# Three pairs of row buffers, a longer lag and a new order in a fused attention and expert kernel

## The chip, the cores and the metric

The kernel runs on one core of one Trainium2 chip. The metric is the device time of one execution in microseconds (us), as the median of the runs shown. The profile is of one further execution; its own time stands beside its span below.

## The reference

Sliding-window attention with a distance bias, then a layer of eight experts whose weights come from eight rounds of row and column balancing. Every token goes through every expert.

```python
q, k, v: (8, 8, 576, 64) float32          # batch, heads, positions, head size
scores = q @ k.T / 8 - slope[head] * |distance|, where 0 <= distance < 128, else -1e9
x = softmax(scores) @ v                    # laid out as (4608, 512)

logits = x @ w_gate                        # (4608, 8)
P = np.exp(logits - logits.max())
for _ in range(8):
    P /= P.sum(1, keepdims=True) + 1e-09
    P /= P.sum(0, keepdims=True) + 1e-09
    P *= N / E
out = 0
for e in range(8):
    h = np.maximum(x @ w1[e], 0.0)         # w1[e]: (512, 1024)
    out += P[:, e:e + 1] * (h @ w2[e])     # w2[e]: (1024, 512)
```

## The kernel before, in words

The kernel schedules itself by hand: the instructions of an engine run in the order in which the program issues them, and an engine that waits holds up what is queued behind it. Semaphores are set from the regions of buffers that are read and written.

The first stage (to about 300 us) is the attention, with the experts 0 and 1 woven in as plain matmuls. Their results go unweighted to a scratch tensor `ysp` in HBM, and the rows of x to another, `xd`. The second stage is the balancing of P. Neither is touched by the change, but for the place of two constants.

The third stage does the experts 2 to 7. Its unit is one group of 256 tokens (two blocks of 128) and one expert: 18 groups of six experts, N = 108 units. `units[n]` gives the group and the expert; the unit's place in its group is n % 6 (NE = 6), place 0 for expert 2 up to place 5 for expert 7. In the first group, experts 6 and 7 (units 4 and 5) run layer 1 plainly. In all others both layers are done by Winograd's form of Strassen's 2x2 product, with seven products in place of eight:

- **Layer 1** (`part`, L983). The x operand of a group is in `xset` (four transposed quarters and four sums of them, made by `sums_x`). The seven products a11, s1, s2, a12, s3, s4, a22 accumulate in three PSUM banks A, B and C, with three copies on ScalarE that carry a partial result on (A to B after a11, C to the SBUF buffer `s5` after s1, B to C after s2). A result is one of four quarters ("slots" 0 to 3) of h. Slot 0 is read from bank A after a12, slot 3 is bank B plus s5 (token `p+`, VectorE, L1027, `add_h`), slot 1 is bank C plus s5 (`c+`), slot 2 is bank B after a22. ScalarE applies the relu with the token's weight P as scale (`relu`, L1013) and leaves 128 x 512 fp16 rows in `hr`.
- **The transposes** (`turn_h`, L1019, issued on SP). `hr` holds four quarters, two pairs: slots 0 and 3, slots 1 and 2. When a pair is complete, one DMA transposes it into `hs[n % 2]`. The same four quarters are written again in the next unit.
- **Layer 2** (`product`, L1071). Five sums of the transposed quarters are made on VectorE (`sum_h`, L1043, tokens t5, t6, t1, t4, t7). The seven products of a unit run in the order 3, 4, 2, 6, 1, 5, 7. Product 3 and product 4 read quarters of the first pair; products 2, 6, 1, 5, 7 read t5, t6, t1, t4, t7. They accumulate over the six experts of a group in PSUM (`sum_of`), in four of five banks that rotate from group to group. Token `X` in a plan is the next product of a single long stream, so the number of X in each plan sets how far layer 2 lags behind layer 1.
- **Gathering** (`gather`, tokens g1 to g7, L1113). When a group's products are complete they are added into `acc`, which `begin` (tokens B0, B1, L1087 and L1091) has started with the weighted results of experts 0 and 1; these come from `ysp` through a buffer y (tokens Y0, Y1, `load_y`, L1081, issued on POOL). `finish` (token FIN) sends acc to the output.
- **The next x** comes by `XL0`, `XL1` (loads from xd on POOL) and `XT0`, `XT1` (transposes on SP), then `SX` (`sums_x`).
- **Weight sums** for the experts (`todo`) are done on VectorE, by tokens W in the first units (`sums_at` says how many at the start of a unit).

A plan is a string of such tokens for one place of a group, written out by hand; `step` carries it out in order:

```python
plans = (
    "a11 X s1 X s2 a12 X s3 p+ s4 c+ t5 X t6 t7 X X t4 a22 X t1",
    ...
```

Token `F` in units 0 and 1 is a piece of the second stage's leftover work. The very last unit has no successor: its layer 2 is done plainly (`plain`, L1133), against rows of expert 7's w2 that are loaded again, because the Strassen sums had replaced a part of them (`load_w2`, eight pieces on POOL).

Of the kernel before, what the change touches and what calls it, by code (L numbers as in the profile page):

```python
# [9 lines left out]
FP16 = mybir.dt.float16  # L10
FP32 = mybir.dt.float32
# [3 lines left out]
def kernel(  # L15
# [10 lines left out]
    nc = tc.nc  # L26
    AF = mybir.ActivationFunctionType
    ALU = mybir.AluOpType
# [52 lines left out]
    ident32 = per.tile([P, P], FP32, name="ident32")  # L81
    ones32 = per.tile([P, P], FP32, name="ones32")
# [169 lines left out]
    if True:  # L252
# [752 lines left out]
        hr = per.tile([P, 4, HF], FP16, name="hr", tag="xT", bufs=4)  # L1005
        hs: dict = {}
        AT = {0: 0, 3: 1, 1: 2, 2: 3}

        def relu(n, slot, src):

            g, e = units[n]
            blk = 2 * g + slot % 2
            nc.scalar.activation(out=hr[:, AT[slot]], in_=src, func=AF.Relu, scale=P_sb[:, blk, e : e + 1])  # L1013

        def turn_h(n, i):

            if n % 2 not in hs:
                hs[n % 2] = per.tile([P, 8, NF2, P], FP16, name=f"hs_{n % 2}", tag="hT", bufs=2)
            nc.sync.dma_start(  # L1019
                out=hs[n % 2][:, 2 * i : 2 * i + 2].rearrange("p s f k -> p (s f) k"),  # L1020
                in_=hr[:, 2 * i : 2 * i + 2].rearrange("p s f -> p (s f)"),
                transpose=True,
            )

        def add_h(n, slot, name):
            to = hr[:, AT[slot]]
            nc.vector.tensor_tensor(out=to, in0=psum(name), in1=s5, op=ALU.add)  # L1027
            relu(n, slot, to)
            if slot == 3:
                turn_h(n, 0)  # L1030
# [52 lines left out]
        def begin(g, e):  # L1083
            for m in range(2):
                blk = 2 * g + m
                if e == 0:
                    nc.vector.tensor_scalar(  # L1087
                        out=acc[:, m, :], in0=y[:, m, :], scalar1=P_sb[:, blk, 0:1], scalar2=None, op0=ALU.mult
                    )
                else:  # L1090
                    nc.vector.scalar_tensor_tensor(  # L1091
                        out=acc[:, m, :], in0=y[:, m, :], scalar=P_sb[:, blk, 1:2], in1=acc[:, m, :],
                        op0=ALU.mult, op1=ALU.add,
                    )
# [32 lines left out]
        def plain(m, name, lo, hi):  # L1127
# [3 lines left out]
            fts = [(f + NF2 * m) % NFT for f in range(NFT)]  # L1131
            for ft in fts:
                nc.tensor.matmul(  # L1133
                    out=ps,
                    lhsT=hs[(N - 1) % 2][:, AT[2 * (ft // NF2) + m], ft % NF2, :],
                    rhs=W2L[e]["all"][:, ft, lo:hi],
                    start=(ft == fts[0]),
                    stop=(ft == fts[-1]),
                )
            a = acc[:, m, lo:hi]  # L1140
# [3 lines left out]
            nc.sync.dma_start(out=out[t0 : t0 + P, lo:hi], in_=a)  # L1144

# [20 lines left out]
        y = s5y[:, 1].bitcast(FP16).rearrange("p (m d) -> p m d", m=2)  # L1166
# [24 lines left out]
        def step(n, plan):  # L1191
            gi = n // NE
            for tok in plan.split():
# [16 lines left out]
                elif tok in ("B0", "B1"):  # L1210
                    begin(groups[gi], int(tok[1]))
# [12 lines left out]
                elif tok in ("Y0", "Y1"):  # L1224
                    load_y(groups[gi], int(tok[1]))
# [15 lines left out]
        )  # L1241
        first = {
# [4 lines left out]
            N - 1: "a11 s1 X B1 s2 X a12 X s3 p+ s4 X c+ t5 X t6 X a22 X t1 t4 g3 X t7 X g4 X g2 X g6 g1 g5 g7",  # L1247
        }
        sums_at = {1: 3, 2: 3, 3: 2, 4: 4, 5: 3, 6: 3, 9: 4, 10: 3}
        for n in range(N):  # L1250
# [3 lines left out]
            if n == 1:  # L1254
# [43 lines left out]
```

## Time and profile before

| | |
|---|---|
| median of 3 runs | 1015.14 us (1015.04 to 1016.08) |
| the profiled execution | 1014.62 us, its span 1012.8 us |
| PE (TensorE matmul) busy | 985.9 us, 97% |
| DVE (VectorE) busy | 685.7 us, 68% |
| ACT (ScalarE) busy | 626.4 us, 62% |
| POOL (GpSimd) busy | 181.0 us, 18% |
| transposes hs<-hr on SP | 216, median 3.2 us from issue to landing |
| loads of y on POOL | 36 of 256 KB, median 3.3 us to landing |
| loads of x rows on POOL | 34 of 128 KB, median 2.7 us to landing |

PEld is the load of TensorE's stationary operand, which runs beside the matmuls. A group line has the line of the kernel, engine, operation and buffers (written<-read), the count, the busy time and the mean of one in ns; a wait line has who waited for whom, us in total, times and the longest. In a timeline line the first two numbers are the start from the span's start and the duration in us, and a square bracket holds the idle time of the engine just before and what ended it. Consecutive instructions of an engine overlap at their ends in this record, so the distance of two starts is what one costs.

### The profile page before, as it was taken

Reading aid. Unit: us, or ns where it says so; the run is one execution under the profiler, and the core shown is the slowest. Engines: PE = TensorE matmul, PEld = TensorE weight load, DVE = VectorE, ACT = ScalarE, POOL = GpSimd, SP = SyncE. Lnnn points to the kernel's source line nnn. Section 1 sums busy time; section 2 is a strip of 40 time slices with the busy share of each in tenths; the row PEclk is TensorE's granted clock in tenths of the full one; section 3 lists DMA queues with packets and bytes.
Section 4 is the critical chain, followed back from the end, with each engine's and each line's share of the span. In section 5 each row is a group of like instructions: output and inputs, shape, how many; then the busy total and the mean of one; then the engine's idle time right before and its main releaser. Section 6 shows DMA issues by size and latency. Waiting matters only on the chain.

```text
span 1012.8 us, 19357 instructions
## 1 busy us (share of the span) xinstructions
PE 985.9 (97%) x7247; PEld 624.6 (62%) x7247; DVE 685.7 (68%) x1546; ACT 626.4 (62%) x1000; POOL 181.0 (18%) x317
## 2 busy tenths in 40 slices
PE   8999999999999999999999999999999999999997
PEld 5645665556544666666666666666666666666655
DVE  5737667665698778676676666666666666677665
ACT  7655645454424656767766666666766666677663
POOL 3324544445100000001000000011100000000011
PEclk9999999999999999999999999999999999999999
DMA  9998899989995656676666655655656656655676
GB/s 244 214 272 219 181 242 222 234 169 183 210 214 130 133 105 131 133 121 125 135 121 125 132 121 120 133 122 120 139 122 124 137 122 130 130 126 120 139 128 115
DMA packets 382877, 155.54 MB, mean 154 GB/s; under 512 B 334720, under 2 KB 372352, under 8 KB 382784
## 3 DMA queue, kind: packets, MB, share of 16 engines
q1 hardware_dynamic: 359680, 110.87, 54.4%
q0 software_dynamic: 22672, 43.27, 19.1%
q8 instruction: 57, 0.93, 0.4%
q14 instruction: 36, 0.29, 0.1%
q10 hardware_dynamic: 432, 0.16, 0.1%
HBM read 78.30 MB, written 23.59 MB: 101 GB/s over the span
## 4 chain that ended last, share of the span: by engine, by line
PE 81%; DMA 11%; DVE 5%; ACT 1%; issue 1%; DVEq 0%; ACTq 0%
PE psM L1071 27%; PE psy L159 12%; PE psB L983 11%; DMA hs<-hr 10%; PE psh L137 9%; PE psA L983 8%; PE psC L983 7%; PE psh L118 3%; DVE hr L1027 2%; PE psS L457 1%; PE psN L491 1%; DMA k<-in_k_dram 1%; DVE hs L1043 1%; DVE pt L468 1%; ACT pt L463 1%
## 5 line engine op out<-in xcount | busy, mean ns | idle before, releaser
L1071 PEld LDWEIGHTS <-hs 128*128 128x128 f16 x2996 | 291.2, 98 | 160.9 <-DVE hs L1043 20.6
L1071 PE MATMUL psM<-w2l,hs 128*128 128x256 f16 x1440 | 216.7, 274 | 12.6 <-DVE hs L1043 11.3
L1013 ACT ACTIVATE hr<-hr,L_sb 128x512 f16<-128x512 f16 x212 | 144.2, 716 | 92.7 <-DVE hr L1027 90.7
L1027 DVE TENSOR_TENSOR hr<-psB,s5y 128x512 f16<-128x512 f32 x106 | 73.3, 692 | 184.2 <-PE psB L983 141.2
L1043 DVE TENSOR_TENSOR hs<-hs 128x512 f16<-128x512 f16 x535 | 192.7, 418 | 1.1 <-DMA hs<-hr 0.4
L983 PEld LDWEIGHTS <-xset 128*128 128x128 f16 x1484 | 144.5, 97 | 76.2 <-issue 4.0
L159 PE MATMUL psy<-w2t,hT 128*128 128x512 f16 x576 | 135.7, 379 | 0.0
L1071 PE MATMUL psM<-more,hs 128*128 128x256 f16 x864 | 126.5, 273 | 0.5 <-DMA hs<-hr 0.5
L983 PE MATMUL psA<-w1l,xset 128*128 128x512 f16 x356 | 105.9, 379 | 0.4 <-ACT hr L1013 0.4
L983 PE MATMUL psB<-s,xset 128*128 128x512 f16 x356 | 105.6, 378 | 0.0
L149 ACT ACTIVATE hT<-psh 128x512 f16<-128x512 f32 (+1 forms) x104 | 60.4, 581 | 70.1 <-PE psh L137 70.0
L137 PE MATMUL psh<-xT,w1t 128*128 128x512 f16 (+1 forms) x448 | 99.0, 364 | 0.0
L463 ACT ACTIVATE pt<-psS 128x1024 f16<-128x1024 f32 x64 | 64.6, 1022 | 50.6 <-PE psS L457 50.1
L1013 ACT ACTIVATE hr<-psA,L_sb 128x512 f16<-128x512 f32 x110 | 76.0, 691 | 26.3 <-DMA hs<-hr 18.3
L159 PEld LDWEIGHTS <-hT 128*128 128x128 f16 x576 | 54.1, 98 | 58.9 <-issue 1.3
L1184 ACT COPY psC<-psB 128x512 f32<-128x512 f32 x106 | 60.4, 570 | 47.3 <-PE psB L983 47.3
L1113 DVE TENSOR_TENSOR acc<-acc,psM 128x256 f32<-128x256 f32 (+1 forms) x162 | 77.4, 506 | 10.5 <-PE psM L1071 7.8
L1027 DVE TENSOR_TENSOR hr<-psC,s5y 128x512 f16<-128x512 f32 x106 | 72.5, 683 | 16.4 <-DMA hs<-hr 12.3
L1180 ACT COPY psB<-psA 128x512 f32<-128x512 f32 x106 | 60.4, 570 | 33.5 <-PE psA L983 33.5
L582 DVE CAST yo<-psy 128x512 f16<-128x512 f32 x65 | 44.6, 689 | 51.2 <-PE psy L159 47.1
L1081 POOL DMA_DIRECT2D s5y<-ysp x36 | 25.9, 720 | 280.7 <-DVE acc L1091 213.5
L1013 ACT ACTIVATE hr<-psB,L_sb 128x512 f16<-128x512 f32 x108 | 72.7, 673 | 2.9 <-PE psB L996 1.1
(133 smaller groups left out, 1167.2 us busy)
## 6 DMA issues: line engine op xcount, KB each, us to landing
s5y<-ysp POOLq DMA_DIRECT2D x36, 256.0 KB, 3.3
ysp<-yo SPq DMA_DIRECT2D x65, 128.0 KB, 4.2
v<-in_v_dram SPq DMA_DIRECT2D x32, 256.0 KB, 4.8
out_dram<-acc POOLq DMA_DIRECT2D x30, 256.0 KB, 3.1
q<-in_q_dram SPq DMA_DIRECT2D x5, 1024.0 KB, 6.6
k<-in_k_dram SPq DMA_DIRECT2D x5, 1024.0 KB, 9.3
xst<-xd POOLq DMA_DIRECT2D x34, 128.0 KB, 2.7
hs<-hr SPq DMA_TRANSPOSE x216, 3.2
```

The costliest lines, as they stand in the source:

```text
L137: nc.tensor.matmul(out=ps[:, 0:nt], lhsT=w1ts[e][:, dt, P * ft : P * ft + P], rhs=xT[:, at : at + nb, dt, :], start=(dt == 0), stop=(dt == ...
L149: nc.scalar.activation(out=st["hT"][:, ft, 0:nt], in_=ps[:, 0:nt], func=AF.Relu)
L159: nc.tensor.matmul(out=ps, lhsT=st["hT"][:, ft, P * ms : P * ms + P], rhs=w2ts[e][:, ft, :], start=(ft == 0), stop=(ft == NFT - 1),)
L463: nc.scalar.activation(out=pt, in_=ps.rearrange("p a y n -> p (a y) n"), func=AF.Exp, scale=scale)
L983: nc.tensor.matmul(out=psum(name), lhsT=xset[n // NE % 2][:, x, P * k : P * k + P], rhs=q[k], start=(start and k == 0), stop=(k == 1), ski ...
L1013: nc.scalar.activation(out=hr[:, AT[slot]], in_=src, func=AF.Relu, scale=P_sb[:, blk, e : e + 1])
L1027: nc.vector.tensor_tensor(out=to, in0=psum(name), in1=s5, op=ALU.add)
L1043: nc.vector.tensor_tensor(out=t[:, AT.get(to, to)], in0=t[:, AT[x]], in1=t[:, AT[y]], op=op)
L1071: nc.tensor.matmul(out=ps, lhsT=hs[n % 2][:, LEFT[m], f, :], rhs=W2L[e][RIGHT[m]][:, f, :], start=(e == 2 and f == 0 and half == 0), stop= ...
L1113: nc.vector.tensor_tensor(out=a, in0=a, in1=p2, op=op)
L1180: nc.scalar.copy(out=psum("B"), in_=psum("A"))
L1184: nc.scalar.copy(out=psum("C"), in_=psum("B"))
```

## The change

- The rows of h: the four quarters of `hr` are cut into two pairs and a third pair is put beside `s5` in the tile `s5y`, where y was. The pair i of unit n is number (2n + i) % 3.
- The lag: unit 1 has two X in place of three. From then on a unit runs five products of the unit before the last and two of the last one. The last unit has twelve.
- y: loaded and used by blocks of 128 tokens (tokens Y00, Y01, Y10, Y11 and B00, B01, B10, B11, expert and block), 72 loads of 128 KB. Three blocks of a group use one buffer `y_e` in turn, in the place that the buffer for x rows had. The x rows' buffer is now the tile of the two constants (identity and ones, no longer needed by then), and the fourth block of y uses it too.
- All plans are written anew: p+ and c+ follow s3 and s4 more closely, the sums t come in another order, the weight sums of unit 0 stand behind its a22, the gathers are drawn from places 1 and 2 mostly into place 1, XL1 follows XT0 at once.
- The plain units 4 and 5 use bank B for slot 2 (before: A).
- The last unit: the plain layer 2 runs in halves, first all that reads the first pair of rows, then all that reads the second; the eight pieces of w2 are loaded in three units (3, 3, 2), not four.

```diff
-    ident32 = per.tile([P, P], FP32, name="ident32")
-    ones32 = per.tile([P, P], FP32, name="ones32")
+    consts = per.tile([P, 2, P], FP32, name="consts")
+    ident32, ones32 = consts[:, 0], consts[:, 1]
...
-        hr = per.tile([P, 4, HF], FP16, name="hr", tag="xT", bufs=4)
+        hr4 = per.tile([P, 4, HF], FP16, name="hr", tag="xT", bufs=4)
+        hr = [hr4[:, 0:2], hr4[:, 2:4]]
...
+        def rows(n, i):
+            return hr[(2 * n + i) % 3]
+        def quarter(n, slot):
+            return rows(n, AT[slot] // 2)[:, AT[slot] % 2]
...
-            nc.scalar.activation(out=hr[:, AT[slot]], in_=src, func=AF.Relu, scale=P_sb[:, blk, e : e + 1])
+            nc.scalar.activation(out=quarter(n, slot), in_=src, func=AF.Relu, scale=P_sb[:, blk, e : e + 1])
...
-                in_=hr[:, 2 * i : 2 * i + 2].rearrange("p s f -> p (s f)"),
+                in_=rows(n, i).rearrange("p s f -> p (s f)"),
...
-            to = hr[:, AT[slot]]
+            to = quarter(n, slot)
...
-        def load_y(g, e):
-            nc.gpsimd.dma_start(out=y, in_=ysp[e, 2 * g : 2 * g + 2].rearrange("m p d -> p m d"))
+        def y_at(e, m):
+            return xst[0] if e == m == 1 else y[0]
+        def load_y(g, e, m):
+            nc.gpsimd.dma_start(out=y_at(e, m), in_=ysp[e, 2 * g + m])
...
-        def plain(m, name, lo, hi):
+        def plain(m, name, fh, lo, hi):
...
-            fts = [(f + NF2 * m) % NFT for f in range(NFT)]
-            for ft in fts:
+            done = name in begun
+            begun.append(name)
+            for f in range(NF2):
...
-        y = s5y[:, 1].bitcast(FP16).rearrange("p (m d) -> p m d", m=2)
+        hr.append(s5y[:, 1].bitcast(FP16).rearrange("p (s f) -> p s f", s=2))
+        y: list = []
...
-                    plain_l1(n, slot, {0: "A", 3: "B", 1: "C", 2: "A"}[slot])
+                    plain_l1(n, slot, {0: "A", 3: "B", 1: "C", 2: "B"}[slot])
...
         plans = (
-            "a11 X s1 X s2 a12 X s3 p+ s4 c+ t5 X t6 t7 X X t4 a22 X t1",
-            "a11 g4 X s1 X g3 s2 g6 X g5 a12 s3 p+ s4 X c+ X X a22 t5 g7 t6 X t4 t1 t7 Y0 XL0",
-            "a11 g2 s1 X g1 FIN X s2 a12 X s3 p+ s4 X c+ X t5 t4 a22 XT0 t6 X X t7 t1 XL1",
-            "a11 X s1 X s2 a12 X s3 p+ s4 c+ X X t5 t6 a22 X XT1 t4 t1 t7 X B0 Y1",
-            "a11 X s1 X s2 a12 X s3 s4 p+ X c+ t5 X a22 X t4 t6 t1 X SX t7",
-            "a11 s1 X X s2 a12 X s3 s4 p+ X c+ X t5 t4 t6 a22 t7 t1 X X B1",
+            "a11 s1 X X s2 X a12 s3 s4 p+ X c+ t5 t6 X a22 X t1 t4 X t7",
+            "a11 s1 X g4 X s2 g3 X a12 g6 s3 X s4 p+ X X c+ a22 g5 X t5 t7 g7 t6 t1 t4 g2 Y00 XL0",
+            "a11 s1 X s2 g1 FIN X X a12 s3 p+ s4 X c+ t5 X a22 XT0 XL1 t6 t1 X X t7 t4",
+            "a11 s1 X X s2 B00 Y01 X a12 s3 s4 p+ c+ t5 X t6 X t4 a22 X t1 X XT1 t7 B01",
+            "a11 Y10 Y11 s1 X X s2 X X a12 s3 p+ s4 c+ X t5 t6 t7 X t4 X a22 t1 SX B10",
+            "a11 X X s1 s2 a12 X X s3 B11 s4 p+ c+ X X X t5 t6 t4 t7 a22 t1",
         )
         first = {
-            0: "a11 s1 W W F s2 a12 F W W s3 p+ s4 c+ F W W a22 F",
-            1: "a11 s1 F s2 a12 F s3 p+ s4 c+ t5 t6 X t1 X t4 a22 X t7 Y0",
-            4: "L0 X X L3 X X L1 t5 X t6 t4 X L2 X SX t7 t1",
-            5: "L0 X X L3 X X L1 t5 X t6 t4 X L2 X B1 t7 t1",
-            N - 1: "a11 s1 X B1 s2 X a12 X s3 p+ s4 X c+ t5 X t6 X a22 X t1 t4 g3 X t7 X g4 X g2 X g6 g1 g5 g7",
+            0: "a11 s1 W W F s2 a12 F s3 s4 p+ c+ F a22 W W F",
+            1: "a11 s1 F s2 a12 F s3 s4 p+ c+ X t5 t6 t1 t4 t7 a22 X",
+            4: "L0 Y10 Y11 X X L3 X X L1 X t5 X t6 t4 L2 t7 t1 X SX B10",
+            5: "L0 X X L3 B11 X X L1 X t5 X t6 t4 L2 t7 t1 X",
+            N - 1: "a11 X s1 s2 a12 B11 X s3 s4 p+ c+ X X a22 X t5 X X t6 t1 t4 g3 X t7 X g4 X g2 X g6 X g1 g5 g7",
         }
-        sums_at = {1: 3, 2: 3, 3: 2, 4: 4, 5: 3, 6: 3, 9: 4, 10: 3}
+        sums_at = {1: 3, 2: 3, 3: 3, 4: 4, 5: 4, 6: 3, 9: 4, 10: 3}
...
-                xst[:] = [per.tile([P, HD], FP16, name="xst", tag="yo", bufs=YO)] * 2
-                step(n, "XL0")
-            if N - NE + 1 <= n < N - 1:
-                for i in range(2):
-                    load_w2(E - 1, 2 * (n - N + NE - 1) + i, 8)
-        plain(1, "A", 0, HD)
-        plain(0, "C", 0, HB)
-        plain(0, "B", HB, HD)
+                y.append(per.tile([P, HD], FP16, name="y_e", tag="yo", bufs=YO))
+                xst[:] = [consts.rearrange("p a n -> p (a n)").bitcast(FP16)] * 2
+                step(n, "Y00 XL0")
+            if N - NE + 1 <= n < N - 2:
+                for i in range(3 * (n - N + NE - 1), min(8, 3 * (n - N + NE))):
+                    load_w2(E - 1, i, 8)
+        plain(1, "A", 1, 0, HD)
+        plain(0, "C", 0, 0, HB)
+        plain(0, "B", 0, HB, HD)
+        plain(1, "A", 0, 0, HD)
+        plain(0, "C", 1, 0, HB)
+        plain(0, "B", 1, HB, HD)
```

More of the change, by code (lines that the diff above doesn't have):

```diff
@@ L1078, in product, with begin @@
                 )
-        def load_y(g, e):
-            nc.gpsimd.dma_start(out=y, in_=ysp[e, 2 * g : 2 * g + 2].rearrange("m p d -> p m d"))
[L1083 to L1094, printed above, removed]
+        def y_at(e, m):
+            return xst[0] if e == m == 1 else y[0]
+        def load_y(g, e, m):
+            nc.gpsimd.dma_start(out=y_at(e, m), in_=ysp[e, 2 * g + m])
+        def begin(g, e, m):
+            blk = 2 * g + m
+            if e == 0:
+                nc.vector.tensor_scalar(
+                    out=acc[:, m, :], in0=y_at(e, m), scalar1=P_sb[:, blk, 0:1], scalar2=None, op0=ALU.mult
+                )
+            else:
+                nc.vector.scalar_tensor_tensor(
+                    out=acc[:, m, :], in0=y_at(e, m), scalar=P_sb[:, blk, 1:2], in1=acc[:, m, :],
+                    op0=ALU.mult, op1=ALU.add,
+                )
         def gather(g, m):
@@ L1125, in finish @@
                         nc.gpsimd.dma_start(out=out[t0 : t0 + TL, :], in_=a[TL * half : TL * half + TL])
-        def plain(m, name, lo, hi):
+        def plain(m, name, fh, lo, hi):
             g, e = units[N - 1]
             ps = psum(name)[:, 0 : hi - lo]
-            fts = [(f + NF2 * m) % NFT for f in range(NFT)]
-            for ft in fts:
+            done = name in begun
+            begun.append(name)
+            for f in range(NF2):
                 nc.tensor.matmul(
                     out=ps,
[L1135 to L1138, printed above, removed]
-                )
+                    lhsT=hs[(N - 1) % 2][:, AT[2 * fh + m], f, :],
+                    rhs=W2L[e]["all"][:, NF2 * fh + f, lo:hi],
+                    start=(not done and f == 0),
+                    stop=(done and f == NF2 - 1),
+                )
+            if not done:
+                return
             a = acc[:, m, lo:hi]
@@ L1209, in step @@
                         gather(groups[last], int(tok[1]))
-                elif tok in ("B0", "B1"):
-                    begin(groups[gi], int(tok[1]))
+                elif tok[0] == "B":
+                    begin(groups[gi], int(tok[1]), int(tok[2]))
                 elif tok == "FIN":
```

5 lines of the change are left out of this document (3 added, 2 removed).

## The prediction

> **What bounds the kernel now.** First the page's busy times and its row of granted clocks, then the waits, then the order of time in one unit that loses time, then the last unit.
>
> ```profile
> PE 985.9 (97%) x7247; PEld 624.6 (62%) x7247; DVE 685.7 (68%) x1546; ACT 626.4 (62%) x1000; POOL 181.0 (18%) x317
> ...
> PEclk9999999999999999999999999999999999999999
> ```
>
> PE is the bound and the others have a third of their time free. So only PE's own pauses can be won. Up to 321 us nothing is changed; all that follows is on the 108 units of the routed stage.
>
> Working of a unit: 7 layer-1 products of 0.43 us (two 512-wide matmuls, the distance of consecutive ones in the timeline) and 7 layer-2 products of 0.437 us (8 matmuls take 0.87 in the chain): 6.08. In the timeline the first psA matmul of a unit comes 6.08 after that of the unit before in most units (708.58, 714.66, 720.74, 726.83). I read off all 108 starts, from 321.65, and took from each unit's length its products at those rates. What is left over:
> - units 0 to 5: 1.1, 0.3, 0.3, 0, 0.55, 0.55 = 2.8
> - eight units between 374 and 531 (every third one): 0.25 to 0.76, sum 4.3
> - twelve between 542 and 815: 0.68 to 1.20, sum 10.4
> - units 102, 103, 105: 0.1, 1.1, 1.3 = 2.5
> - unit 107, the last: 15.49 for 11.45 of work = 4.0
>
> Sum 24.0. The direct sum agrees: from 321.65 to the last matmul's end at 1009.26 are 687.6, the work is 663.6.
>
> ```profile
> DVE hr L1027 <- DMA hs<-hr: 35.2, 23, 4.5
> ...
> PEld L1071 <- DVE hs L1043: 20.6, 26, 2.5
> ...
> ACT hr L1013 <- DMA hs<-hr: 18.3, 17, 2.2
> ...
> PE psM L1071 <- DVE hs L1043: 11.3, 15, 2.0
> ```
>
> PE waits for the sums of layer 2's left sides (L1043); VectorE, which makes them, and ScalarE wait for transposes still reading hr. Unit 47's pause, in order of time:
>
> ```profile
> 618.62 9.49 SPq L1019 DMA_TRANSPOSE hs<-hr  x4
> ...
> 624.28 0.59 PE L983 MATMUL psB<-w1t,xset 128*128 128x512 f16 x2
> ...
> 624.83 0.69 DVE L1027 TENSOR_TENSOR hr<-psC,s5y 128x512 f16<-128x512 f32 x1 [0.91 <-DMA hs<-hr]
> 625.44 1.76 DVE L1043 TENSOR_TENSOR hs<-hs 128x512 f16<-128x512 f16 x5
> ...
> 625.91 0.33 PEld L1071 LDWEIGHTS <-hs 128*128 128x128 f16 x4 [0.88 <-DVE hs L1043]
> 625.91 0.61 PE L1071 MATMUL psM<-w2l,hs 128*128 128x256 f16 x4 [0.60 <-DVE hs L1043]
> ```
>
> ```profile
> 619.95 4.79 DMA hs<-hr
> ...
> DMA to landing us min/median/max: 3.0/3.2/6.4
> ```
>
> The second transpose of unit 46 lands 4.79 us after 619.95, at 624.74. Until then c+ may not overwrite those rows of hr; t5 is queued behind c+, and the product that reads t5 is next on PE. With the median landing of 3.2 there is no pause. In the units that pause from 374 to 815 the chain has mostly 4.2 to 5.2.
>
> The last unit:
>
> ```profile
> 999.00:1001.70 2.70, 0.74 (x5) 0.22 (x3) 1.05 (x4) 1.02 (x2) 0.00 (x0) 1.00 0.27 53
> 1001.70:1003.00 1.30, 1.24 (x9) 1.05 (x10) 1.27 (x4) 1.00 (x2) 0.00 (x0) 0.78 0.49 91
> 1003.00:1004.00 1.00, 1.00 (x7) 0.69 (x5) 1.00 (x3) 0.00 (x0) 0.00 (x0) 0.50 0.06 12
> 1004.00:1005.40 1.40, 1.40 (x8) 0.98 (x7) 1.26 (x4) 0.00 (x0) 0.00 (x0) 0.50 0.94 179
> ```
>
> PE waits 2.0 us for t5 (its transposes take 5.8 and 6.4 in the chain, beside the pieces of w2 issued at 978.14 and 990.32), and the granted clock, the number before the last two, then drops to 0.50: 2.2 of wait, 1.8 of slow products.
>
> The Trainium skill (TensorE: Matmul & The Clock Gate, The HAM clock gate) lets the clock fall only after an idle window of about 3.4 us. By that rule a 2 us wait costs itself alone, and the last unit would give back 2.2 and not 4.0; the trace disagrees here, and it decides.
>
> **The change, part by part.**
>
> *Three pairs and the lag.* A pair of rows is now written again three turns later and not two. So c+ waits for the first transpose of the unit before (p+ starts 3.73 into it, its relu ends by 5.2; 4.8 more is 3.9 into the next unit, where c+ is not ready before 4.3), and a12's relu for one that is a unit older: the waits for hs<-hr (35.2 and 18.3) go. Unit n now does five products of n-2 and two of n-1, and those two read only the first pair. A t-sum is made in one unit and first read in the next. What is late next is t5 where a22 stands last (places 4 and 5 of a group; a22 starts 5.64 into the unit). From a22's start to its transpose are 1.76 (618.19 to 619.95), so issue at 7.40. Landing at 3.2: 10.60, which is 4.52 into the next unit, when c+ is just done. Landing at 4.8: 6.12; t5 (0.42) is done at 6.54, and its product stands third in the unit after, at 6.08 + 0.87 = 6.95. So the usual slow landing is covered with 0.4 to spare; the fifth sum (1.76 for five) ends at 7.88 and the product t1 feeds starts at 8.25. Credit: 0.3 + 4.3 + 10.4 + 2.5 = 17.5.
>
> *Sums moved in units 0 and 1.* The two W sums (1.29) of unit 0 stood before p+, which started at 327.25 though psB was done at 325.70; a22 came 1.1 late. Behind a22 they hold up nothing: 1.1. In unit 1 p+ follows three sums and a cast; I leave the 0.3 standing.
>
> *Plain units 4 and 5.* Slot 2 goes to bank B, so the next unit's first product need not wait for the relu of bank A (361.52, 0.69 long): 0.55 twice = 1.1. Bank B is not written again before 1.7 us later.
>
> *The last unit.* The w2 pieces go out by unit 105, and all eight are issued before the last units' transposes, so I take 3.2 for these. Walking the new order at 0.43 a product: the last of the twelve ends at 8.25, and the first pair, issued at 4.85, has landed at 8.05; its halves (1.74) end at 9.99, and the second pair, issued at 6.2, has landed at 9.4. No wait. If both land at 4.8, up to 1.4 us. I credit 3.5 of 4.0.
>
> *y by blocks.* Same bytes in twice the loads (POOL has 18% busy; an issue is 0.55). New is the queue: the block for B01 is issued behind XL1, and XL1 waits for the first x transpose to land. XT0 goes out at 7.7 of place 2 and lands 3.08 later (722.57 to 725.65); behind XL1's issue the block's starts at 11.33. Page rows land in 2.7 (128 KB) to 3.3 (256 KB): 14.63, or 2.5 into place 4. VectorE stands in B01 until then, 0.44 more is 2.9; p+ behind it is wanted at 4.16, and a22 lets it start as late as 4.85. Zero, covered by 1.9. The second x block and B11 end likewise at 3.5 of place 5 against 4.16. Cover gone, each costs its lateness once a group.
>
> *Gathers pulled into place 1.* Nine operations: 1.80 for three, 0.75 for a pair (711.38). In place 1 VectorE gets 3.3 of them beside p+ and c+ (1.2, by their distance) and the five sums (1.7): 6.2 for 6.08. The next place asks 3.5. Zero, with 0.1 to 0.5 a group if anything else is late. In unit 10, where three weight sums stand behind B01, 0.3 once.
>
> Nowhere does a number of matmuls, relus or bytes change.
>
> **The sum.** Won: 17.5 + 1.1 + 1.1 + 3.5 = 23.2. New small waits: 1.2 (0.3 in unit 10, the rest for places with under 0.5 of slack). Net 22.0: 1014.6 of the profiled execution becomes 992.6. The median of the runs shown lies 0.5 above that execution: 993.1. Bounds: all 24.0 gone, 991.1; 0.3 more in each of 17 groups, 998. The span is 1012.8, 1.8 less than that execution's time; I take what lies around it as unchanged.
>
> **The rivals.**
> 1. *The sums still come late.* If the slow landings grow to the longest seen, 6.4, t5 at places 0 and 5 ends at 8.1 against 6.95: 1.2 each, or 0.8 at 6.0. For: 5.8 and 6.4 exist. Against: only beside w2 pieces; from 815 to 960 no landing made PE wait. In half of the pausing 25 units, 0.8 each: 10 us, 1003. The Trainium skill (DMA: Bandwidth & Descriptors, Queues, rings and completion order) has each DMA engine take turns between its queues packet by packet, so a load in flight stretches a transpose; the two long landings above agree.
> 2. *VectorE becomes the bound at place 1.* 0.5 a group over 17 groups is 8.5: 1001.6. For: 6.2 against 6.08. Against: the surplus is carried into a place with 2.5 free.
> 3. *The y queue, slower than before.* The block for B01 lands so late that p+ and a22 slip in every group. It costs the lateness less 1.9, 17 times, and undoes the gain of 22 from 1.3 a group on, that is from 3.2 later than walked. With 5.3 for the x transpose (the row xset<-acc) and 4.8 for the block (the 128 KB row of w2t): 2.2 + 1.5 - 1.9 = 1.8, 31 us, 1024. For: three transfers in a row. Against: the x transposes that I followed took 3.04 to 3.08.
> 4. *The third pair brings nothing*, because it shares a tile with s5 and is ordered with it: only units 0, 4, 5 and the end gain 5.7, 1009.4. Against: in the built order the s5 copy waits for PE alone.
>
> **Chances.** Forecast 0.74; sums 0.08; VectorE 0.08; y queue 0.07; third pair 0.03. The range 990.5 to 1003.5 holds the forecast's own (990.5 to 998) and the first two rivals. A measurement of this kernel tells 0.2% (2 us) from no change. Faster by more: all but the y queue, 0.93; within: 0.02 of its 0.07 (lateness that just eats the gain); slower: its other 0.05.
>
> **What would show it.** Right: no wait of VectorE or ScalarE for hs<-hr, PE's wait for L1043's successor under 3 us in all, units 6.08 apart from 374 to 990, no stretch below full clock before the last matmul. Wrong: waits of the adds for psC behind an acc operation (y), of PE for the sums in places 0 and 5 (landings), or in place 2 (gathers). A time above 1000 would mean one of these; above 1013, that y's queue decides.

## The result, and the profile after

| | before | after |
|---|---|---|
| median | 1015.14 us (5 runs, 1011.80 to 1016.63) | 998.32 us (5 runs, 998.0 to 1003.9) |
| ratio, with its 95% interval | | 0.9848 (0.9816 to 0.9879) |
| the profiled execution, its span | 1014.62, 1012.8 | 998.06, 996.3 |
| third stage, first product to last | 687.6 | 672.6 |
| of it without a product | 24.0 | 9.0 |

The change gains 16.8 us by the medians; 22 were forecast. The median lies 0.3 us above the forecast's own part of the range (990.5 to 998), in the part that was kept for the first two rivals. In the last two rows the third stage runs from the start of the first product of unit 0 to the end of the last matmul, and 663.6 of it is the work that the prediction worked out. I compare kernels by these rows, because the stages ahead are the same in all of them, but their length is not: in the profiled executions below the third stage begins anywhere from 320.0 to 324.3 us. It began 1.66 us earlier in the profile of after than in that of before. So of the 16.6 us between the two profiled executions 15.0 lie in the third stage.

The page of after, busy times and granted clock:

```profile
PE 979.4 (98%) x7247; PEld 626.0 (63%) x7247; DVE 687.3 (69%) x1546; ACT 625.5 (63%) x1000; POOL 192.6 (19%) x353
...
PEclk9999999999999999999999999999999999999999
```

The waits of after:

```profile
DVE acc L1097 <- DMA y_e<-ysp: 41.2, 17, 4.0
...
DVE hr L1035 <- DMA hs<-hr: 2.8, 1, 2.8
PEld L1079 <- DVE hs L1051: 2.6, 4, 1.7
...
PE psM L1079 <- DVE hs L1051: 1.2, 1, 1.2
```

VectorE's 23 waits for transposes still reading hr (35.2 us) have become one of 2.8, ScalarE's are gone, and TensorE's waits for the sums fell from 20.6 and 11.3 to 2.6 and 1.2. New is the wait of VectorE for blocks of y, 41.2 us in 17 groups.

The stretch from 362 to 940 us as a whole (its length, then the busy time of TensorE, weight loads, VectorE, ScalarE and POOL; the third number from the end is the clock). Before:

```profile
362.00:940.00 578.00, 567.72 (x3887) 377.69 (x3887) 392.35 (x907) 398.16 (x649) 57.77 (x97) 1.00 0.62 127
```

After:

```profile
362.00:940.00 578.00, 574.70 (x3962) 386.58 (x3960) 401.75 (x923) 403.60 (x659) 70.14 (x130) 1.00 0.64 129
```

TensorE is idle for 10.3 us of it before (578.00 less 567.72) and for 3.3 after. In starts of products, the measure of the prediction, the pauses of after are: unit 1, 0.2; unit 2, 0.4; 394 to 431, three, 1.4; 686 to 691, three, 2.1; 720 to 723, two, 1.3; units 105 and 106, 3.3; unit 107, 0.2. Those of units 105 and 106, in the timeline of after:

```profile
964.12 1.31 SPq L1027 DMA_TRANSPOSE hs<-hr  x1
965.52 3.79 SPq L1027 DMA_TRANSPOSE hs<-s5y  x1
...
966.42 0.55 POOL L1092 DMA_DIRECT2D y_e<-ysp  x1 [1.18 <-DVE acc L1097]
...
972.18 1.05 PE L1079 MATMUL psM<-more,hs 128*128 128x256 f16 x8 [1.83 <-DMA hs<-hr]
972.23 0.69 DVE L1035 TENSOR_TENSOR hr<-psC,s5y 128x512 f16<-128x512 f32 x1 [2.81 <-DMA hs<-hr]
...
975.26 1.05 PE L1079 MATMUL psM<-w2l,hs 128*128 128x256 f16 x8 [1.17 <-DVE hs L1051]
```

and in its chain:

```profile
965.52 9.23 DMA hs<-s5y
```

The two transposes of unit 104, issued at 964.12 and 965.52, landed after 8.02 and 9.23 us. Between 963.60 and 967.47 POOL issued five pieces of w2 and a block of y, 128 KB each. The last unit, in contrast, has no wait at all (the first plain product, L1144, follows without a bracket):

```profile
988.11 1.04 PE L1079 MATMUL psM<-w2l,hs 128*128 128x256 f16 x8
988.99 1.03 PE L1144 MATMUL psA<-w2t,hs 128*128 128x512 f16 x4
```

### The profile page after: what moved, and what is told of

Same layout as the page of the kernel before. It is cut to its first block, busy times and chain, and to the rows that moved or that the text cites. A ratio compares the mean times of both kernels' runs of the same rounds, so it can differ in the third digit from the quotient of the medians.

```text
span 996.3 us, 19438 instructions
## 1 busy us (share of the span) xinstructions
PE 979.4 (98%) x7247; PEld 626.0 (63%) x7247; DVE 687.3 (69%) x1546; ACT 625.5 (63%) x1000; POOL 192.6 (19%) x353
## 4 chain that ended last, share of the span: by engine, by line
PE 88%; DMA 6%; DVE 3%; ACT 1%; issue 1%; SPq 1%; POOL 0%; DVEq 0%; POOLq 0%; ACTq 0%
PE psM L1079 30%; PE psB L983 13%; PE psy L159 12%; PE psh L137 9%; PE psA L983 8%; PE psC L983 8%; PE psh L118 3%; DMA hs<-s5y 2%; PE psN L491 1%; PE psS L457 1%; DMA xset<-consts 1%; DMA v<-in_v_dram 1%; DMA consts<-ysp 1%; DVE pt L468 1%; ACT psB L1196 0%
## 5 line engine op out<-in xcount | busy, mean ns | idle before, releaser
L1079 PE MATMUL psM<-w2l,hs 128*128 128x256 f16 x1440 | 195.6, 273 | 1.2 <-DVE hs L1051 1.2
L1021 ACT ACTIVATE hr<-hr,L_sb 128x512 f16<-128x512 f16 x142 | 98.4, 716 | 59.1 <-DVE hr L1035 57.8
L1079 PE MATMUL psM<-more,hs 128*128 128x256 f16 x864 | 121.0, 273 | 1.8 <-DMA hs<-hr 1.8
L1035 DVE TENSOR_TENSOR hr<-psB,s5y 128x512 f16<-128x512 f32 x71 | 49.0, 691 | 94.0 <-PE psB L983 93.2
L468 DVE TENSOR_TENSOR pt<-pt,mask 128x1024 f16<-128x1024 f16 x64 | 52.1, 814 | 30.4 <-ACT pt L463 30.4
L1198 ACT COPY s5y<-psC 128x512 f32<-128x512 f32 x106 | 62.7, 591 | 6.5 <-PE psC L983 6.5
L137 PEld LDWEIGHTS <-w1t 128*128 128x128 f16 x448 | 41.3, 98 | 37.5 <-issue 0.6
L1131 POOL DMA_DIRECT2D out_dram<-acc x30 | 16.3, 548 | 247.0 <-DVE acc L1123 247.0
```

The source lines that it names most:

```text
L137: nc.tensor.matmul(out=ps[:, 0:nt], lhsT=w1ts[e][:, dt, P * ft : P * ft + P], rhs=xT[:, at : at + nb, dt, :], start=(dt == 0), stop=(dt == ...
L468: nc.vector.tensor_tensor(out=pt, in0=pt, in1=mask_of[kb][:, 4 * u : 4 * u + 4, :], op=ALU.mult)
L1021: nc.scalar.activation(out=quarter(n, slot), in_=src, func=AF.Relu, scale=P_sb[:, blk, e : e + 1])
L1079: nc.tensor.matmul(out=ps, lhsT=hs[n % 2][:, LEFT[m], f, :], rhs=W2L[e][RIGHT[m]][:, f, :], start=(e == 2 and f == 0 and half == 0), stop= ...
L1198: nc.scalar.copy(out=s5, in_=psum("C"))
```

## The experiments

### One part of the change at a time

Two pairs with everything else of the change (`two_pairs`):

```diff
-            return hr[(2 * n + i) % 3]
+            return hr[i]
```

> The changed kernel with rows(n, i) returning hr[i], so the two pairs of before; lag, plans and y stay as changed. Theory A (pairs and lag work on the same wait, and either covers a landing of 4.8 us by itself): VectorE and ScalarE wait for hs<-hr again, 20 to 50 us in all, since c+ may come only after the second transpose of the unit before (issued up to 7.4 into it, landed 4.5 to 6.1 into the next, c+ ready at 4.3); but the sums have a unit's time, so PE's waits for them grow by 2 to 6 us only: 1000 to 1004. Theory P (the third pair carries the gain): the pauses of before return, about 14 us: 1010 to 1014.

Measured: 1011.12 us (1008.91 to 1011.74), 0.9973 (0.9958 to 0.9987) of before; third stage 681.6, of it 18.0 lost. Its waits:

```profile
DVE hr L1035 <- DMA hs<-hr: 20.2, 16, 5.4
PEld L983 <- issue: 17.5, 33, 2.5
ACT hr L1021 <- DMA hs<-hr: 17.4, 13, 3.5
```

The lag alone keeps TensorE clear of the sums, but VectorE's c+ and ScalarE's relu still wait for the old rows, ScalarE's copy of bank A to B comes late behind the relu, and the pause moves to layer 1.

Three pairs with the old plans and the old lag, but y by blocks (`old_plans`; the tokens of y are put where the old plans allow):

```diff
-            "a11 s1 X X s2 X a12 s3 s4 p+ X c+ t5 t6 X a22 X t1 t4 X t7",
+            "a11 X s1 X s2 a12 X s3 p+ s4 c+ t5 X t6 t7 X X t4 a22 X t1",
...
-        sums_at = {1: 3, 2: 3, 3: 3, 4: 4, 5: 4, 6: 3, 9: 4, 10: 3}
+        sums_at = {1: 3, 2: 3, 3: 2, 4: 4, 5: 3, 6: 3, 9: 4, 10: 3}
```

> The changed kernel with three pairs, but with the plans and weight-sum counts of before (lag of four products; only the y tokens are those of the change). Theory A: with c+ free, t5 starts when the transpose lands (624.74 in the unit shown) and is done when its product stands next (625.31), so the pauses of 0.7 to 1.2 us shrink to 0.2 or less; unit 0 loses its 1.1 again and the last unit about 1: 1000 to 1004. Theory P: the same or 998. Theory L (the lag carries the gain): 1009 to 1014, with PE's wait for the sums at 10 us or more.

Measured: 1013.04 us (1009.91 to 1017.5), 0.9993 (0.9972 to 1.0015); third stage 687.5, lost 23.9.

```profile
DVE acc L1097 <- DMA y_e<-ysp: 32.8, 17, 3.7
DVE acc L1101 <- DMA consts<-ysp: 16.6, 11, 3.0
...
PEld L1079 <- DVE hs L1051: 13.4, 30, 3.8
...
DVE hr L1035 <- DMA hs<-hr: 2.1, 1, 2.1
```

Here the waits for hr are nearly gone (2.1) and the sums are still read in the unit that makes them. So the theory that either part alone covers a late landing fell. From 362 to 940 us, where the late landings are, TensorE is idle for 10.3 us in before, for 8.8 with two pairs, for 8.0 with the old plans and for 3.3 with both parts. In the whole third stage the third pair is worth 9.0 us where the lag is there (18.0 to 9.0), and the new plans 14.9 where the third pair is there (23.9 to 9.0). Alone the plans win 6.0 of the stage (24.0 to 18.0; 2.7 by the ratio to before) and the third pair 0.1. These stage figures hold more than the two parts: units 105 and 106, where pieces of w2 meet the transposes (below), lose 7.3 us with the old plans and 4.1 with two pairs, half clock behind a wait included, and 3.3 in the changed kernel; and the old plans bring back the 1.1 of unit 0.

### Where the y queue stands

XL1 behind Y01, so that the first block of y no longer waits for the x transpose (`y_first`):

```diff
-            ... c+ t5 X a22 XT0 XL1 t6 t1 X X t7 t4",
-            "a11 s1 X X s2 B00 Y01 X a12 ...
+            ... c+ t5 X a22 XT0 t6 t1 X X t7 t4",
+            "a11 s1 X X s2 B00 Y01 XL1 X a12 ...
```

> The changed kernel with XL1 behind Y01 in place 3 and not at the end of place 2, so that the y block no longer stands behind a load that waits for an x transpose. Theory Q (queue order on POOL holds VectorE in B01 and B11): VectorE's 41 us of waits for y_e<-ysp fall under 10, and the 2.1 us lost at 684 to 692 and the 1.2 at 719 to 723 go: 995 to 997. Theory D (these places lose time because loads and transposes share the DMA engines): waits for y shrink too, but PE's waits there stay within 1 us of what they are: 997.5 to 998.5.

Measured: 1004.76 us (1001.98 to 1009.3), 0.9918 (0.9888 to 0.9948); third stage 679.3, lost 15.7: slower than the changed kernel. Its waits:

```profile
POOL y_e L1092 <- DVE acc L1097: 100.3, 35, 23.6
POOL y_e L1092 <- DVE acc L1101: 38.6, 17, 2.7
DVE acc L1101 <- DMA consts<-ysp: 28.4, 16, 3.4
```

B01 waits no longer, but the second x block, its transpose and Y11 behind it are now 5 us later: Y11 goes out beside the transposes of hs and lands after 4.1 us in the median and not 2.5, and B11 waits for it in 16 groups. The queue passes its lateness on to whatever stands last in it.

The adds of y behind c+ (`late_b`, on top of the w2 pieces 4, 1, 3 below):

```diff
-            ... a22 X t1 X XT1 t7 B01",
-            "a11 Y10 Y11 s1 X X s2 X X a12 s3 p+ s4 c+ X ... SX B10",
-            "a11 X X s1 s2 a12 X X s3 B11 s4 p+ c+ ... a22 t1",
+            ... a22 X t1 X XT1 t7",
+            "a11 Y11 s1 X X s2 X X a12 s3 p+ s4 c+ B01 Y10 X ... SX",
+            "a11 X X s1 s2 a12 X X s3 s4 p+ c+ B11 ... a22 t1 B10",
...
```

> The kernel with the 4, 1, 3 pieces and the adds of y moved behind c+: B01 from the end of place 3 to behind c+ of place 4, Y10 behind it and Y11 ahead of it, B11 behind c+ of place 5, B10 to the end of place 5. Theory Y (where the block of y lands late, B01 keeps p+ and so the relus waiting; seen as 41.2 us of waits of VectorE for y, of which about 1.6 us came through to TensorE around 720 us): VectorE's wait for y falls from 49 to under 15 us and the pauses of 714 to 727 go: 1 to 2 us under the kernel with the 4, 1, 3 pieces. Rival (VectorE has nothing to do in that time, and the sums t5 in places 4 and 5 come 0.4 to 0.9 later now): no gain, or 0.3 a group slower, up to 5 us.

Measured: 999.68 us (996.01 to 1001.53), 0.9868 (0.9846 to 0.9889); third stage 672.1, lost 8.5, where the kernel that it starts from loses 5.4 and 6.6 in its two runs. The wait went (under 3 us in all), the time did not:

```profile
DVE hs L1051 <- DMA hs<-hr: 7.0, 9, 2.0
PEld L1079 <- DVE hs L1051: 6.6, 11, 2.0
...
PEld L1079 <- DMA hs<-s5y: 3.9, 4, 1.2
```

Y10 goes out later and now runs beside the transposes of place 4; 52 of 194 transposes land after 4 us or more (42 in both runs of the kernel with the pieces 4, 1, 3) and TensorE waits for these. The rival's number came: no gain. What VectorE's wait cost by itself this run doesn't tell, because the edit moved loads with it.

No loads of y after the first group (`no_y`; the first group's blocks are added again in all later groups):

```diff
                 elif tok[0] == "Y":
-                    load_y(groups[gi], int(tok[1]), int(tok[2]))
+                    if gi == 0:
+                        load_y(groups[gi], int(tok[1]), int(tok[2]))
```

> The changed kernel without the loads of y after the first group (the later groups add the first group's blocks again; 68 loads of 128 KB are left out). Theory Y: the pauses in the group that sends four stores (686 to 691, 2.1 us), at 720 (1.6) and a part of the 3.3 at 965 to 974 go, as the loads share the DMA engines with transposes and B01 no longer waits: 994 to 996. Rival (the transposes are long for the x loads, the stores and the w2 pieces, and y costs nothing): 997.5 to 999, with the same pauses.

Measured: 1001.77 us (998.66 to 1002.35), 0.9883 (0.9858 to 0.9908); third stage 672.2, lost 8.6. The total hides three things. In the profiled execution the third stage begins at 324.3 us, 4.3 later than in that of after. From 362 to 940 us the pauses are gone:

```profile
362.00:940.00 578.00, 577.93 (x3994) 389.86 (x3992) 403.89 (x929) 407.58 (x665) 36.22 (x67) 1.00 0.56 116
```

So all that TensorE loses there in the changed kernel, 3 to 5 us, comes from the loads of y. But units 105 and 106 lose 7.7 us instead of 3.3: without B01 and its block in POOL's queue, the five pieces of w2 go out within 2.1 us, and in the view of DMA issues from 962 to 976 us (median us to landing last) stands

```profile
w2t<-in_moe_w_dram POOLq DMA_DIRECT2D x5, 128.0 KB, 8.2
...
hs<-s5y SPq DMA_TRANSPOSE x1, 10.2
```

TensorE waits for these transposes, 4.8 us in starts of products, and 2.8 of the 7.7 come behind the wait, at half clock (the third number from the end):

```profile
973.48:980.30 6.82, 5.77 (x22) 3.30 (x23) 2.85 (x7) 2.45 (x4) 0.00 (x0) 0.50 0.55 104
```

### The pieces of w2

The eight pieces as 4, 1, 1, 2 behind units 103 to 106 (`w2_spread`), as 4, 1, 3 (`w2_413`, run twice) and as 4, 0, 4 (`w2_404`):

```diff
-                for i in range(3 * (n - N + NE - 1), min(8, 3 * (n - N + NE))):
+                at = (0, 4, 4, 8)[n - N + NE - 1 :]
+                for i in range(at[0], at[1]):
```

> The changed kernel with the eight pieces of w2 loaded as 4, 1, 1 and 2 after units 103, 104, 105 and 106, not as 3, 3 and 2 after 103 to 105. Theory W (five pieces and a y block together stretch the transposes of unit 104 to 8.0 and 9.2 us, and PE pays 3.3 us): those transposes land within 5 us, PE's two waits at 970 and 974 fall under 1 us in all, 995 to 996. Rival (the pieces cost the same wherever they are): the waits move to units 103 or 106, 997.5 to 998.5.

> The changed kernel with the pieces of w2 issued 4, 1 and 3 after units 103, 104 and 105 (changed kernel: 3, 3, 2); all eight are still out ahead of the last unit's transposes. In the changed kernel the two transposes of unit 104 landed after 8.02 and 9.23 us, beside five pieces and one block of y issued within 4 us, and TensorE lost 3.3 us to them. Theory W (these loads stretch the transposes): unit 104's transposes land within 5 us, the 3.3 go, and the last unit stays free of waits (in the spread 4, 1, 1, 2 the last two pieces took 2.5 there): 3 us under the changed kernel's 998.3, 994.5 to 996. Rival (the store of the finished group, which is issued just before, stretches them): unit 104 loses the same 3 us, 997.5 to 999.

> The changed kernel once more, on one chip with the two below, since profiled executions of one kernel or of kernels that are the same up to 320 us began the third stage anywhere from 320.0 to 324.3, which is more than the 3.7 us that the pieces of w2 move in that stage (672.6 from its first product to the last in the changed kernel, 669.0 with the pieces 4, 1, 3). Theory W: about 672.6 in the stage again, unit 104's transposes over 7 us again, and a median of 998 to 1000. Rival (the 8 and 9 us were an accident of one execution): the stage takes 669 to 670 and the three medians agree.

> The kernel with the w2 pieces 4, 1, 3 once more, beside the changed kernel. Theory W: third stage 669 to 670.5, unit 104's transposes under 5.5 us, and the median 2 to 3.7 under the changed kernel's. If its last unit's transposes land at 3.2 this time (they took 4.95 and 4.38 with no load in flight but one packet of instructions): 667.5. Rival: no difference.

> The pieces of w2 4, 0, 4: none with unit 104's transposes, four behind unit 105, which must land before the last unit's transposes. Theory W: as 4, 1, 3 or up to 0.5 better in the stage, unit 104's transposes at 3.2 to 4.2, unit 105's at up to 5 with no pause from them; 668 to 670. Rival (the pieces behind unit 105 then delay the last unit's): a wait of 1 to 2 us of the plain products, 670 to 671.

| kernel | median us (range) | ratio to before, interval | stage, lost | unit 104's transposes landed after | lost in units 105, 106 | wait of the last unit |
|---|---|---|---|---|---|---|
| after | 998.32 (998.0 to 1003.9) | 0.9848 (0.9816 to 0.9879) | 9.0 | 8.0, 9.2 | 3.3 | 0 |
| after_2 | 1003.46 (997.42 to 1004.51) | 0.9881 (0.9857 to 0.9904) | 7.0 | 7.9, 8.8 | 2.9 | 0 |
| w2_spread | 998.34 (996.02 to 1001.4) | 0.9852 (0.9826 to 0.9879) | 7.3 | 4.7, 4.8 | 0 | 1.3 |
| w2_413 | 999.13 (994.95 to 1001.39) | 0.9862 (0.9839 to 0.9884) | 5.4 | 4.8, 4.8 | 0 | 1.5 |
| w2_413_2 | 1000.3 (997.73 to 1001.72) | 0.9869 (0.9850 to 0.9887) | 6.6 | 4.6, 5.2 | 0 | 0 |
| w2_404 | 997.53 (996.42 to 998.59) | 0.9836 (0.9820 to 0.9853) | 6.3 | 3.8, 3.3 | 0 | 1.1 |

The same view of DMA issues from 962 to 976 us, for w2_404:

```profile
w2t<-in_moe_w_dram POOLq DMA_DIRECT2D x4, 128.0 KB, 4.7
...
hs<-hr SPq DMA_TRANSPOSE x4, 4.1
hs<-s5y SPq DMA_TRANSPOSE x1, 3.3
```

Every kernel with fewer pieces issued by the time of unit 104's transposes loses nothing in units 105 and 106. Both executions of the changed kernel lose 3 there, the other kernels with the old spread (`two_pairs`, `old_plans`, `y_first`, `old_end`) 2.5 to 7.3, and no_y, with the loads closer together, most. This is shown: the pieces stretch the transposes. The stores of the finished group are issued just ahead in all of them and do no harm. Only the last three rows and after_2 were measured on one chip; there 4, 0, 4 is the fastest, with an interval that ends at 0.9853 where that of the changed kernel begins at 0.9857. It is the fastest version here, by an amount that the runs don't settle: six executions of the changed kernel on that chip lie in two clusters, at 997 to 999 and at 1003 to 1005, and the profile is of one in the lower cluster. What the upper one does differently stays open. `w2_413` was expected at 994.5 to 996 and took 999.13: the 3.3 us went from units 105 and 106, but the median doesn't show it.

### The last unit

The plain products not halved, as before (`old_end`):

```diff
-        plain(1, "A", 1, 0, HD)
-        plain(0, "C", 0, 0, HB)
-        plain(0, "B", 0, HB, HD)
-        plain(1, "A", 0, 0, HD)
-        plain(0, "C", 1, 0, HB)
-        plain(0, "B", 1, HB, HD)
+        plain(1, "A", 0, HD)
+        plain(0, "C", 0, HB)
+        plain(0, "B", HB, HD)
```

> The changed kernel with the last unit's plain layer 2 not halved (all of block 1 first, starting with the second pair of rows, as before). The second pair landed at 990.37 and the products before end at 989.0: by the walk of the prediction a wait of 1.4 us and no more, 999.7. Rival (a wait just before the end also lets the granted clock fall to half, as 2.0 us did in the kernel before): 1.4 and up to 1.8 more, 1000 to 1001.5, and granted clock under 0.9 in the last unit. If the transposes land at 3.1 beside no wait at all, 998.3.

Measured: 1001.41 us (998.77 to 1004.22), 0.9889 (0.9865 to 0.9912); third stage 676.2, lost 12.6, of which the last unit's wait is 1.05 and the rest lies in groups that the edit doesn't touch. The clock stays at 1.00 through the wait and after it (timeline by stretches):

```profile
994.00:996.00 2.00, 1.11 (x9) 0.56 (x8) 1.76 (x5) 0.00 (x0) 0.00 (x0) 1.00 0.65 135
996.00:998.00 2.00, 2.00 (x14) 1.22 (x13) 1.84 (x5) 0.00 (x0) 0.00 (x0) 1.00 0.00 0
```

A wait near 1 us, as first expected, and no clock drop behind it. The whole time doesn't price the halves better than that.

### What makes a transpose slow

The landings of before that cost time, 4.2 to 5.2 us, were read as given in the prediction. The packets of the trace say where they come from. Two stretches of before's DMA queues, around the second transpose of unit 46 (issued 619.95, landed 624.74). Its data:

```profile
DMA packets 899, 0.22 MB, mean 186 GB/s; under 512 B 899, under 2 KB 899, under 8 KB 899
...
q1 hardware_dynamic: 899, 0.22, 99.0%
```

that is from 621.4 to 622.6; and from 622.6 to 623.6:

```profile
q8 instruction: 1, 0.02, 5.5%
q1 hardware_dynamic: 8, 0.00, 0.8%
```

At 622.68 one packet of 16 KB of queue q8 starts and takes 0.88 us. Two small packets of the transpose come only at 623.5, behind it; all the rest was done by 622.7. That these share a DMA engine with the fetch is read from the times; the trace doesn't name the engine of a packet. Of the transpose's 16 completion counts 15 had come 3.2 us after its issue, and the last came at 4.79, 1.16 us after its last packet, where transposes without a fetch have some 0.5. So 0.88 us on the queue make 1.6 at the landing, and why the last part is so long stays open. q8 carries TensorE's instructions: the page has 57 such packets, 0.93 MB, and 14,494 records of matmuls and weight loads (two times 7247), which is 64 bytes each; from one packet to the next TensorE starts some 255 instructions, which is three units, and the pauses of before come every third unit. Of the 34 transposes between 362 and 960 us into which such a packet fell (1.05 to 3.4 us after issue) 29 landed after 4.0 us or more; of the 158 others 5 did, at 4.12 at most. The pauses missing from before's list, near 715, 752 and 790, belong to three of the other five, which landed in 3.06 to 3.11; in the one that I followed the packet started at 755.34, after the transpose's last data (755.1).

To test it, I left the kernel before as it was and put 56 idle instructions of TensorE into the second stage, 4.0 us of a unit's pace, so that every later fetch falls elsewhere (`shift`; its lines stand two further down):

```diff
+        for _ in range(28):
+            nc.tensor.matmul(out=psM2, lhsT=w1ts[0][:, 0, 0:P], rhs=w1ts[0][:, 0, 0:1])
         nc.tensor.matmul(out=psM2, lhsT=ones32[0:1, :], rhs=mx_sb[0:1, 1:2])
```

> The kernel before, with nothing of the change, and 28 idle one-column matmuls (56 more instructions on TensorE) ahead of the matmul of L867 in the second stage; their result is overwritten. Theory F: the slow landings are those into which a fetch of TensorE's instructions falls. In the trace of before a packet of 16 KB of the instruction queue comes once in some 255 TensorE instructions, three units, and takes 0.9 to 1.6 us on its DMA engine; of the 34 transposes hs<-hr from 362 to 960 us with such a packet starting 1.05 to 3.4 us after their issue, 29 landed after 4.0 us or more, of the 158 others 5 did (4.0 to 4.1). 56 instructions are 4.0 us of a unit's pace, so every fetch comes 4.0 us earlier against the units: 8 to 10 transposes are hit and not 34. Then the pauses of units 6 to 81 (14.7 us) fall to under 5, and the third stage from its first product to its last takes 676 to 679 us and not 687.6; whole time 1004 to 1007 with 1 to 3 us for the added matmuls. Rival (the transposes are slow for what their place in the group brings, loads of x and y or SP's queue, and the fetch only goes along with it): the pauses stay where they were in the units, 685 to 689, and the whole time is 1014 to 1017.

Measured: 1000.98 us (998.94 to 1006.41), 0.987 (0.9845 to 0.9895); third stage 672.2, lost 8.6, more than the theory asked for (676 to 679). Fetches hit 3 of 196 transposes and not 34 of 192; 6 landed after 4.0 us or more. The stretch from 362 to 940 us:

```profile
362.00:940.00 578.00, 577.87 (x3989) 389.35 (x3989) 399.23 (x927) 405.32 (x666) 58.80 (x98) 1.00 0.61 130
```

0.1 us of pauses, against 10.3 in the same kernel without the idle matmuls, which cost 0.84 us themselves:

```profile
270.64 0.84 PE L868 MATMUL psM<-w1t 128*128 128x1 f16 x28
```

So the fetches cause the pauses of before, and the kernel before, with its two pairs and its old plans, takes the third stage in the time of the changed kernel when hardly any fetch meets a transpose. The rival (the place in the group makes the transposes slow) fell.

What the change does is then a cover. In after 35 of 196 transposes still land after 4.0 us or more, 34 of 192 in before, and TensorE is idle for 3.3 us over them and not for 10.3. Either part alone leaves most of that: 35 of 192 are late and 8.8 us idle with two pairs, 50 of 192 and 8.0 with the old plans. But the late landings of after are not those of before. Only 13 of the 35 have a fetch in the stretch named above; of the 164 transposes without one 22 are late, where 5 of 158 were in before. In no_y 22 of 197 are late, 14 of them with a fetch, and TensorE pauses for 0.1 us from 362 to 940. So there the cover holds against all late landings behind a fetch, and what after still loses in that stretch comes from its own loads of y. Whether the changed kernel gains more from a moved fetch was not run.

## Why the prediction was right, and where it was off

- **Pairs and lag, 17.5.** The mechanism held. The pauses of 374 to 815, 14.7, fell to 4.8 (3.3 in the second profile). The walk covered landings of 4.8 with 0.4 to spare, so up to 5.2. The first rival's longer ones came in two units: 5.92 us at 425, with 0.8 lost, and 6.05 and 5.50 at 682 and 683, in one of the two groups that send four stores, with 2.1 lost there together with a late B11. The third rival's queue (B11 or B01 waits for its block and keeps p+ waiting) lost 0.7 at 394 to 397 and, in the other group with four stores, 1.3 at 720. The chain of after for B11 in the group of 682:

```profile
682.26 5.42 DMA consts<-ysp
687.68 0.03 issue
687.71 0.03 DVE acc L1101
```

- **y by blocks, zero.** The step failed in its size. It walked the queue and asked when a block lands; it did not ask what a block does to a transpose that lands beside it. no_y prices both, the late blocks and the transposes beside them, at all of the pauses from 362 to 940, 3 to 5 us; 1.2 were forecast for all new waits.
- **Units 102 to 106, 2.5 of the 17.5.** Here the credit failed whole. It took the pauses there as sums read late. The edit that puts three pieces of w2 behind units 103 and 104 was costed only for the last unit, and five pieces and a block of y now meet the two transposes of unit 104: 3.3 us are lost, where 2.5 were lost before and nothing was to be left. The trace of before had the sign: the 1.3 lost in unit 105 came behind a transpose of 5.83 us, issued at 979.42 beside two pieces of w2. w2_404, w2_spread and both runs of w2_413 have nothing there.
- **Units 0 and 1, 1.1, and plain units, 1.1.** As forecast: nothing is left in unit 0, 0.2 of the 0.3 in unit 1, and nothing in units 4 and 5. The 0.3 of unit 2, which the pairs and the lag were to win, stayed (0.4).
- **Last unit, 3.5 of 4.0.** All but 0.2 of the 4.0 came: the transposes landed in 3.07 and 3.10, no wait, no slow clock. In w2_413 and w2_404 the last unit does wait, 1.5 and 1.1, with landings of 4.95 and 4.5; an instruction packet falls into these stretches, as in the section above. So this term hangs on where a fetch falls, and that nearly all of it came is luck. Of the two landings that the prediction names for the last unit of before only the 6.4 is its own; the 5.8 is that of unit 104, and the last unit's other one took 5.32.
- **The residue.** 2.0 forecast, 9.0 found: 7.0 too few, 3.3 of them in units 105 and 106 and 3.6 from 362 to 940 (4.8 found, 1.2 forecast). Of the 7.0, 1.66 came back by the earlier start, which the change didn't bring. That is the 5.4 between 992.6 and 998.06.
- **The other rivals.** VectorE as the bound at place 1: no, with no_y TensorE pauses for 0.1 us in 578 with the same gathers. The third pair brings nothing: no, 5.5 us from 362 to 940 (8.8 to 3.3 us idle).
- **What the prediction took as given.** It asked how late a transpose may land and never why it lands late. With that question the trace of before had the answer ready (a landing every third unit, a packet every third unit), and a rival that undoes the need for the change: 28 idle matmuls.

## What to carry to other kernels

Before restructuring around a transfer that is sometimes late, find what makes it late: line its packets up with the queues that you don't issue, and move one against the other. A cover and the removal of a cause can be worth the same. Here the cover held against the 14 late landings behind a fetch in no_y, though not in the last unit of w2_413 and w2_404; the shift was tried at one place only, and moves again with every instruction added. And cost each load that is moved by what it does to the transfers that it will fly beside, not only by when it lands itself.

## What the runs showed of the hardware

- A fetch of TensorE's code is one packet of 16 KB, 0.88 to 1.9 us long in before, once in some 255 instructions. The 29 transposes of before that were late with one landed after 4.2 to 5.2 us and not 3.2; in the one shown, two of some 1,050 packets came behind it. The Trainium skill (DMA: Bandwidth & Descriptors, Queues, rings and completion order) lets an engine change queues only at the end of a packet; the trace agrees, with the two packets that start as the fetch's 0.88 us end.
- Loads stretch transposes, far more when more of them go out close together: unit 104's two transposes, 3.2 us in most units, took 4.8 and 4.8 beside four pieces of w2 and a block of y issued over 4.4 us (w2_413), 8.0 and 9.2 beside five and a block over 3.9 us (after), 10.9 and 10.2 beside five over 2.1 us (no_y). When the second transpose was issued one, three and four of these pieces were out. Number and spacing weren't varied apart.
- The granted clock. After TensorE's idle times of 1.95 us and more, as the timelines give them, half clock came in all cases past the first 20 us: 2.02 (before, last unit), 2.29 (two_pairs, 982.61), 1.95 (old_plans, 983.22), 2.42 (old_end, 23.27) and 4.66 (no_y); it lasted 3.4 or 6.8 us. After those up to 1.93 none came: 1.83 in after at 972.18, and 1.93 in shift, at nearly the place of the one in before, where the clock stays at 1.00:

```profile
985.00:986.50 1.50, 0.00 (x0) 0.00 (x0) 1.05 (x3) 0.33 (x1) 0.00 (x0) 1.00 0.49 97
986.50:988.00 1.50, 1.47 (x14) 1.32 (x15) 1.47 (x4) 0.97 (x2) 0.00 (x0) 1.00 0.42 77
```

  With so few cases, and 1.93 beside 1.95, that isn't shown to be a threshold. By the rule of the Trainium skill that the prediction cites (TensorE: Matmul & The Clock Gate, The HAM clock gate), waits of some 2 us are too short; shift agrees with it, the four cases from 1.95 to 2.42 do not.
- One kernel's executions differ by up to 7 us (997.42 to 1004.51) with the same program; the profiles of the kernels run here begin the third stage up to 4.3 us apart. The rest stays open.
